# Five rooms instead of three for the first loads, and the low parts of x and of two weight groups summed by TensorE

## The chip, the cores and the metric

The kernel runs on one core of one Trainium2 chip. The metric is the device time of one execution in microseconds (us), the median of the timed runs. The profile is that of one execution, recorded by the hardware profiler.

## The reference

```python
def _attn_ref(q, k, v, alpha):                  # each (4, 8, 768, 48): batch, heads, time, head size
    state = np.zeros((B, H, D, D))
    for t in range(S):
        state = alpha[:, :, t, :, None] * state + np.einsum('bhd,bhe->bhde', k[:, :, t], v[:, :, t])
        y[:, :, t] = np.einsum('bhd,bhde->bhe', q[:, :, t], state)
...
def reference(...):
    x = np.ascontiguousarray(attn_out.transpose(0, 2, 1, 3)).reshape(B * S, H * D)   # (3072, 384)
    h = x @ w_in                                # w_in (384, 2048), float64
    g = np.maximum(0.01 * h, h)
    return (g @ w_out).astype(np.float32)       # w_out (2048, 384), float64
```

## The kernel before

**Two stages that overlap.** The attention is computed in 24 units: 4 batches by 6 time blocks of 128 tokens. The feed-forward part (FFN) has 16 weight groups `f` of 128 hidden columns and 8 token blocks `i` of three units each. `attention(0, AHEAD)` issues the first nine units (AHEAD = 9) ahead of the FFN; the other fifteen are spread between the FFN's matrix products later on. The rows below call the first nine units the head.

**A unit.** Its alpha, q, k and v (192 KB each) come by SP's DMA queue. TensorE transposes alpha, q and k (`transposed`, L280: four matmuls each, which write a PSUM bank of one of two kinds, `a` and `b`, in turn). VectorE (DVE) makes running products of alpha (L314, L320) and scales q (L339, `qs`) and k (L347, `ks`). TensorE makes the scores (`scores`, L356): for each of four head pairs one matmul on the rows 0 to 47 into one bank and one on the rows 64 to 111 into another, 16 records of a matmul in all, because a plain float32 matmul leaves two records. ScalarE (ACT) copies the two banks to `sm` (L366) and GpSimd (POOL) masks them (L367). `k_tokens` (L380) transposes `ks`. `outputs` adds old state times q (L395, from unit 4 on) and values times masked scores (L401) into a bank `y`, and makes the new key-value products (`kv`, L412). ACT rounds `y` to the high part of x (L418, `xh`, type float32r) and DVE subtracts it to give the low part (L419, `xl`).

**The weights.** `converting(f)` turns a group of float64 weights, read as pairs of 32-bit words, into a high part `hi` and a low part `lo` of float32r: two ACT operations (L245, L254) and six DVE operations, of which the last three form `val - hi` (L260), the remaining bits `rest` (L262) and `lo = rest + val` (L265). The first three groups are converted within the head, each behind the marks in the tables AFTER and BEGIN; the others run between the FFN's products.

**The FFN.** `ffn_in` (L493) is nine matmuls of 384 columns into a bank `ph` (hi by xh, hi by xl, lo by xh for three row blocks), then ACT and DVE work on the result; `ffn_out` (L520) is nine matmuls for each block and group.

**What sets the order.** A tile scheduler orders each engine's instructions; `behind(...)` and `put(...)` pin some to others. Each of alpha, q and k has two rooms in SBUF and a third in `spare` for the head's units, and the values have three rooms (NV). `load_next` issues the load of the unit that takes a room as soon as the room's user has been transposed; `load_values(u + NV)` stands at the end of `outputs(u)`. SP issues its transfers in order, and a transfer whose room is not free yet holds all those behind it. The table LOADS puts the weights of the first groups between them.

Of the kernel before, what the change touches and what calls it, by code (L numbers as in the profile page):

```python
# [9 lines left out]
F32 = mybir.dt.float32  # L10
F32R = mybir.dt.float32r
I32 = mybir.dt.int32
U32 = mybir.dt.uint32
I64 = mybir.dt.int64
AF = mybir.ActivationFunctionType
ALU = mybir.AluOpType
# [6 lines left out]
def gated_linear_attn_ffn(ctx, tc, q, k, v, alpha, w_in, w_out, out):  # L23
    nc = tc.nc
# [3 lines left out]
    P = 128  # L28
# [23 lines left out]
    NL = 2, 2, 2  # L52
    NV = 3
    NBITS, NPW, NRAW = 2, 1, 4
    T4 = 4
    RUN = T4 * D
    PITCH = RUN + GAP
    AHEAD = 3 * UPB
    LAG = 3
    SOON, EARLY = 2, 3  # L60
    LEAD = 8
# [29 lines left out]

    spare = pieces("spare", F32, *[(NP * PITCH,)] * 3)
    x_sb, = pieces("large", F32R, (3 * (NG + 1), 2, TB))
# [18 lines left out]
    def places(u, i):  # L112
        return loads_sb[i] + [spare[i]] if u < AHEAD else loads_sb[i]

# [3 lines left out]
    def load_next(u, i):  # L118

        for n in range(u + 1, u + 4):  # L120
            if n < NU and n - len(places(n, i)) == u:
                load(n, i)
# [4 lines left out]
    def load(u, i):  # L127
# [16 lines left out]
        for a in range(4):  # L144
# [4 lines left out]
            )  # L149

    def load_values(u):
        if u >= NU:
            return
        if u >= AHEAD and later is not None:
# [3 lines left out]
        made["v", u] = nc.sync.dma_start(  # L158
            vals_sb[u % NV].rearrange("t (h d) -> t h d", h=H),
            v[b, :, tb * C:(tb + 1) * C, :].rearrange("h t d -> t h d"),  # L160
# [4 lines left out]
    for i in (0, 1, 2):  # L165
        for t in places(0, i):
            nc.vector.memset(by_token(t)[:, :, D:], 1.0)
    for n in range(3):
        for i in range(3):
            load(n, i)  # L170
        if n < NV - 1:
            load_values(n)

# [7 lines left out]
    keep_warm(6)  # L181
    make_identity(nc, ident)
    nc.gpsimd.memset(mask, 1.0)
    nc.gpsimd.affine_select(
# [41 lines left out]
    def converting(f, ordered=False):  # L226
# [31 lines left out]
        put(ordered, "DVE", lambda: nc.vector.tensor_scalar(pw, bits, -0x800000, None, ALU.bitwise_and))  # L258
        yield
        put(ordered, "DVE", lambda: nc.vector.tensor_tensor(val, val, hi.bitcast(F32), ALU.subtract))  # L260
        yield
# [123 lines left out]
    def outputs(u):  # L385
        tb, b = units[u]
        i, j = divmod(u, UPB)
        pe, qs, ktok = live[u][:3]
        V, W = vals_sb[u % NV], state[b]
        at = i % 3 * (NG + 1)  # L390
# [16 lines left out]
        if tb < NC - 1:  # L407
            kv = bank()[:, 0:NP * D].rearrange("d (p e) -> d p e", p=NP)
            for p in range(NP):
                for s, lo, m in ((0, 0, HB), (1, HB, D)):  # L410
# [3 lines left out]
                    )  # L414
        load_values(u + NV)
        live[u] = pe, kv
        xh, xl = (x_sb[0:BR, at:at + NP, n, j * C:(j + 1) * C] for n in (0, 1))
        made["xh", u] = nc.scalar.copy(xh, y[0:BR])  # L418
        made["x", u] = nc.vector.tensor_tensor(xl, y[0:BR], xh.bitcast(F32), ALU.subtract)  # L419

# [133 lines left out]
    for n, _ in enumerate(st):  # L554
        if n == 2:
            load_values(NV - 1)
        while LOADS and LOADS[0][0] in made:
# [188 lines left out]
```

## Time and profile before

| what | value |
|---|---|
| timed runs | 530.58, 530.69, 531.53 us; median 530.69 us |
| span of the profiled execution | 530.9 us |
| TensorE (PE) busy | 518.5 us, 98% |
| VectorE (DVE) busy | 379.0 us, 71% |
| ScalarE (ACT) busy | 230.7 us, 43% |
| GpSimd (POOL) busy | 62.6 us, 12% |
| DMA | 46.64 MB in all, mean 88 GB/s |

The span runs from the first to the last instruction of the profiled execution; it lies 0.2 us above the median of the timed runs, so what is added to or taken from the span can be added to or taken from the time. The ends of matmuls are modelled, so busy time of TensorE overstates its work where matmuls overlap; the times at which they start are recorded. PEld is TensorE's loading of weights, which overlaps its matmuls.

### The profile page before, as it was taken

To read this page: it belongs to the slowest core of one execution; us is meant where nothing else is said; L and a number is where in the kernel's file an instruction comes from. 1 tells how busy PE (TensorE), PEld (TensorE's weight loads), DVE (VectorE), ACT (ScalarE), POOL (GpSimd) and SP (SyncE) were. 2 spreads that over 40 slices of the span, in tenths; PEclk is the share of its full clock that TensorE was granted. 3 is DMA by queue.
4 is the path that set the end of the run, shared out by engine and by line. 5 is a ranking of instruction groups with operands and counts; after the bars stand their busy time and mean duration, and the time that the engine had idled before them with its cause. 6 is when DMAs were issued, how large, how long until landed. Compare 5 with 4: busy or idle time off the path is not lost.

```text
span 530.9 us, 9962 instructions
## 1 busy us (share of the span) xinstructions
PE 518.5 (98%) x3778; PEld 500.0 (94%) x3778; DVE 379.0 (71%) x695; ACT 230.7 (43%) x489; POOL 62.6 (12%) x143
## 2 busy tenths in 40 slices
PE   8997999999999999999999999999999999999995
PEld 7886999999999999999999999999999999999995
DVE  6998899999999997777577586585786534333331
ACT  2764855555534444444334444345344444333331
POOL 4554500000000111100101101101010000000000
PEclk9998999999999999999999999999999999999998
DMA  9999975545726533552251431433201000101001
GB/s 144 168 175 170 229 172 133 131 122 141 170 45 184 127 84 81 102 134 49 60 111 30 112 83 44 92 74 86 54 15 25 31 16 1 23 1 44 1 0 51
DMA packets 92982, 46.64 MB, mean 88 GB/s; under 512 B 57856, under 2 KB 90112, under 8 KB 92928
## 3 DMA queue, kind: packets, MB, share of 16 engines
q1 hardware_dynamic: 92928, 45.93, 39.5%
q8 instruction: 32, 0.52, 0.4%
q14 instruction: 22, 0.18, 0.1%
HBM read 38.83 MB, written 4.72 MB: 82 GB/s over the span
## 4 chain that ended last, share of the span: by engine, by line
PE 87%; DVE 7%; DMA 4%; issue 1%; SPq 0%; DVEq 0%; ACT 0%
PE ph L493 35%; PE b L520 32%; PE a L356 4%; PE a L401 3%; PE a L520 3%; DMA small<-in_v_dram 3%; PE a L395 3%; PE a L412 2%; PE b L401 1%; PE a L380 1%; PE b L280 1%; DMA small<-in_alpha_dram 1%; DVE pw L262 1%; DVE gl L505 1%; DVE t L499 1%
## 5 line engine op out<-in xcount | busy, mean ns | idle before, releaser
L493 PE MATMUL ph<-large,w 128*128 128x384 f32 x1152 | 226.6, 338 | 0.5 <-DVE t L499 0.5
L493 PEld LDWEIGHTS ph<-large,w 128*128 128x128 f32 x1152 | 200.1, 188 | 2.8 <-DVE t L499 1.1
L520 PE MATMUL b<-w,gh 128*128 128x384 f32 x672 | 168.9, 340 | 0.0
L499 DVE TENSOR_TENSOR t<-ph,t 128x384 f32<-128x384 f32 x128 | 70.7, 553 | 79.1 <-ACT t L496 78.9
L520 PEld LDWEIGHTS b<-w,gh 128*128 128x128 f32 x672 | 119.4, 188 | 2.1 <-issue 0.4
L496 ACT ACTIVATE t<-ph 128x384 f32<-128x384 f32 x128 | 62.5, 489 | 128.2 <-PE ph L493 128.2
L501 ACT CAST gh<-t 128x384 fp32r<-128x384 f32 x128 | 65.7, 513 | 119.6 <-DVE t L499 119.6
L520 PE MATMUL b<-w,gl 128*128 128x384 f32 x336 | 107.4, 335 | 0.0
L505 DVE TENSOR_TENSOR gl<-t,gh 128x384 fp32r<-128x384 f32 x128 | 70.9, 554 | 34.3 <-ACT gh L501 34.2
L520 PEld LDWEIGHTS b<-w,gl 128*128 128x128 f32 x336 | 62.6, 188 | 0.0
L367 POOL TENSOR_SCALAR_AFFINE_SELECT sm<-sm 128x512 f32<-128x512 f32 x33 | 23.1, 712 | 207.8 <-ACT sm L366 207.8
L356 PEld LDWEIGHTS a<-qs,ks 48*128 48x128 f32 x312 | 24.1, 188 | 5.1 <-issue 4.2
L356 PE MATMUL a<-qs,ks 48*128 48x128 f32 x312 | 28.7, 285 | 0.0
L289 DVE STREAM_TRANSPOSE ks<-small 128x512 f32<-128x512 f32 x15 | 16.7, 1123 | 14.6 <-PE a L380 14.6
L324 POOL COPY pe<-pc 128x4 f32<-128x4 f32 x24 | 4.8, 202 | 163.7 <-DVE pc L314 163.7
L373 POOL TENSOR_TENSOR small<-us,pe 48x192 f32<-48x192 f32 x40 | 22.4, 560 | 1.5
L314 DVE TENSOR_TENSOR_SCAN pc<-e,small 128x128 f32<-128x128 f32 x60 | 20.4, 401 | 0.0
L366 ACT COPY sm<-a 128x512 f32<-128x512 f32 x24 | 14.0, 583 | 14.0 <-PE b L356 12.9
L520 PE MATMUL a<-w,gh 128*128 128x384 f32 x96 | 19.6, 337 | 0.0
L320 DVE TENSOR_TENSOR_SCAN rc<-e,small 128x511 f32<-128x511 f32 x15 | 19.1, 1276 | 0.2
L401 PE MATMUL a<-sm,small 128*48 128x128 f32 x256 | 17.7, 277 | 0.0
L254 ACT CAST w<-bits 128x768 fp32r<-128x768 f32 x16 | 13.4, 838 | 8.4 <-DVE bits L251 7.8
(92 smaller groups left out, 554.4 us busy)
## 6 DMA issues: line engine op xcount, KB each, us to landing
raw<-in_moe_w_out_dram SPq DMA_DIRECT2D x16, 384.0 KB, 3.8
small<-in_v_dram SPq DMA_DIRECT2D x24, 192.0 KB, 3.7
raw<-in_moe_w_in_dram SPq DMA_DIRECT2D x32, 144.0 KB, 4.0
out_dram<-o SPq DMA_DIRECT2D x24, 192.0 KB, 2.0
small<-in_alpha_dram SPq DMA_DIRECT2D x32, 96.0 KB, 2.3
small<-in_q_dram SPq DMA_DIRECT2D x30, 96.0 KB, 2.4
small<-in_k_dram SPq DMA_DIRECT2D x30, 96.0 KB, 2.2
small<-in_alpha_dram SPq DMA_DIRECT2D x30, 80.0 KB, 2.4
```

Of the source, the lines that this page charges most:

```text
L314: nc.vector.tensor_tensor_scan(pc[:, p, :], aT[:, p, :], ones.broadcast_to([P, C]), 1.0, ALU.mult, ALU.mult)
L320: nc.vector.tensor_tensor_scan(flat[2][:, NP * C - 2::-1], flat[0][:, NP * C - 1:0:-1], flat[1][:, NP * C - 2::-1], last, ALU.mult, ALU.add)
L356: nc.tensor.matmul(ss[s][:, p, :], ks[lo:lo + D, p, :], qs[lo:lo + D, p, :], start=True, stop=True)
L367: made["mask", u] = nc.gpsimd.affine_select(out=sm[s], in_=sm[s], compare_op=ALU.is_ge, fill=0.0, base=0, pattern=[[0, NP], [1, C]], chann ...
L373: nc.gpsimd.tensor_tensor(*scalings.pop(0))
L401: nc.tensor.matmul(y[lo:lo + m, p, :], V[:, c:c + m], masked[u][s][:, p, :], start=not tb and p == 0, stop=p == NP - 1, skip_group_check=True,
L493: nc.tensor.matmul(ph, w_in_of(f, wn, g), xt[:, g, :], start=n == 0, stop=n == 3 * NG - 1)
L496: put(ordered, "ACT", lambda: nc.scalar.mul(t, ph, 0.01))
L499: put(ordered, "DVE", lambda: nc.vector.tensor_tensor(t, ph, t, ALU.max))
L501: put(ordered, "ACT", lambda: nc.scalar.copy(gh, t))
L505: made["gl", i, f] = put(ordered, "DVE", lambda: nc.vector.tensor_tensor(gl, t, gh.bitcast(F32), ALU.subtract))
L520: product = nc.tensor.matmul(po[j], gt[:, js], w_out_of(f, wn), start=f == 0 and n == 0, stop=f == NF - 1 and n == 2)
```

## The change

The nine units' alpha, q and k get three spare rooms each (NS), so five rooms, and the values four more (NVS), so seven. At the start the loads of five units are issued in place of three; `values(u)` chooses a value room. `minus`, a negative identity of type float32r, is made on POOL. For the head's units the low part of x is no longer subtracted by DVE: TensorE adds `minus` times `xh` into the bank `y`, and ACT copies what is left. For the weight groups 0 and 1 (SUMS = 2) `lo` is summed by TensorE in two halves of 384 columns into a bank `ph`: identity times `val`, `minus` times `hi`, identity times `rest`, and ACT copies the sum. The two identity products are plain float32 matmuls, the product with `minus` is float32r. DVE sets the constant columns of six more rooms.

```diff
--- before.py
+++ after.py
@@ -51,12 +51,14 @@
 
     NL = 2, 2, 2
     NV = 3
+    NS, NVS = 3, 4
     NBITS, NPW, NRAW = 2, 1, 4
     T4 = 4
     RUN = T4 * D
     PITCH = RUN + GAP
     AHEAD = 3 * UPB
     LAG = 3
+    SUMS = 2
     SOON, EARLY = 2, 3
     LEAD = 8
     SL = 8 * UPB
@@ -89,7 +91,9 @@
     state, vals_sb, rest = rest[:B], rest[B:B + NV], rest[B + NV:]
     loads_sb = [[rest.pop(0) for _ in range(n)] for n in NL]
 
-    spare = pieces("spare", F32, *[(NP * PITCH,)] * 3)
+    spare = pieces("spare", F32, *[(H * HB,)] * (3 * NS), *[(DM,)] * NVS)
+    spare_sb = [[spare.pop(0) for _ in range(NS)] for _ in range(3)]
+    minus, = pieces("minus", F32R, (P,))
     x_sb, = pieces("large", F32R, (3 * (NG + 1), 2, TB))
 
     w_sb = {}
@@ -110,14 +114,14 @@
         return tc.issue_after(made[key].ins) if key in made else nullcontext()
 
     def places(u, i):
-        return loads_sb[i] + [spare[i]] if u < AHEAD else loads_sb[i]
+        return loads_sb[i] + spare_sb[i] if u < AHEAD else loads_sb[i]
 
     def loaded(u, i):
         return places(u, i)[u % len(places(u, i))]
 
     def load_next(u, i):
 
-        for n in range(u + 1, u + 4):
+        for n in range(u + 1, u + 3 + NS):
             if n < NU and n - len(places(n, i)) == u:
                 load(n, i)
 
@@ -148,6 +152,15 @@
                 src[b, a // 2::2, ts, :].rearrange("p (j t) d -> j p (t d)", t=T4)[:, :, off:],
             )
 
+    def values(u):
+        rooms = vals_sb + spare if u < AHEAD else vals_sb
+        return rooms[u % len(rooms)]
+
+    def load_more_values(u):
+        for n in (u + NV, u + NV + NVS):
+            if (n < AHEAD) == (n > u + NV):
+                load_values(n)
+
     def load_values(u):
         if u >= NU:
             return
@@ -156,7 +169,7 @@
             return
         tb, b = units[u]
         made["v", u] = nc.sync.dma_start(
-            vals_sb[u % NV].rearrange("t (h d) -> t h d", h=H),
+            values(u).rearrange("t (h d) -> t h d", h=H),
             v[b, :, tb * C:(tb + 1) * C, :].rearrange("h t d -> t h d"),
         )
 
@@ -165,11 +178,10 @@
     for i in (0, 1, 2):
         for t in places(0, i):
             nc.vector.memset(by_token(t)[:, :, D:], 1.0)
-    for n in range(3):
+    for n in range(2 + NS):
         for i in range(3):
             load(n, i)
-        if n < NV - 1:
-            load_values(n)
+        load_values(n)
 
     idle = ps_h.tile([P, 512], F32, name="ph")
 
@@ -180,6 +192,7 @@
 
     keep_warm(6)
     make_identity(nc, ident)
+    nc.gpsimd.tensor_scalar(minus, ident, -1.0, None, ALU.mult)
     nc.gpsimd.memset(mask, 1.0)
     nc.gpsimd.affine_select(
         out=mask, in_=mask, compare_op=ALU.is_ge, fill=0.0, base=0,
@@ -257,6 +270,15 @@
         rest = pw.bitcast(F32)
         put(ordered, "DVE", lambda: nc.vector.tensor_scalar(pw, bits, -0x800000, None, ALU.bitwise_and))
         yield
+        if f < SUMS:
+            nc.vector.scalar_tensor_tensor(rest, low.bitcast(U32), 2.0 ** -52, rest, ALU.mult, ALU.mult)
+            for cs in (slice(0, DM), slice(DM, 2 * DM)):
+                ps = ps_h.tile([P, 512], F32, name="ph")[:, 0:DM]
+                nc.tensor.matmul(ps, ident, val[:, cs], start=True, stop=False)
+                nc.tensor.matmul(ps, minus, hi[:, cs], start=False, stop=False)
+                nc.tensor.matmul(ps, ident, rest[:, cs], start=False, stop=True)
+                made["w", f] = nc.scalar.copy(lo[:, cs], ps)
+            return
         put(ordered, "DVE", lambda: nc.vector.tensor_tensor(val, val, hi.bitcast(F32), ALU.subtract))
         yield
         put(ordered, "DVE", lambda: nc.vector.scalar_tensor_tensor(
@@ -386,7 +408,7 @@
         tb, b = units[u]
         i, j = divmod(u, UPB)
         pe, qs, ktok = live[u][:3]
-        V, W = vals_sb[u % NV], state[b]
+        V, W = values(u), state[b]
         at = i % 3 * (NG + 1)
         y = banks4()
 
@@ -412,11 +434,15 @@
                     made["kv", u] = nc.tensor.matmul(
                         kv[lo:lo + m, p, :], ktok[:, p, lo:lo + m], V[:, h * D:(h + 1) * D], start=True, stop=True
                     )
-        load_values(u + NV)
+        load_more_values(u)
         live[u] = pe, kv
         xh, xl = (x_sb[0:BR, at:at + NP, n, j * C:(j + 1) * C] for n in (0, 1))
         made["xh", u] = nc.scalar.copy(xh, y[0:BR])
-        made["x", u] = nc.vector.tensor_tensor(xl, y[0:BR], xh.bitcast(F32), ALU.subtract)
+        if u < AHEAD:
+            nc.tensor.matmul(y[0:BR], minus[0:BR, 0:BR], xh, start=False, stop=True, skip_group_check=True)
+            made["x", u] = nc.scalar.copy(xl, y[0:BR])
+        else:
+            made["x", u] = nc.vector.tensor_tensor(xl, y[0:BR], xh.bitcast(F32), ALU.subtract)
 
     def next_state(u):
         tb, b = units[u]
@@ -553,7 +579,8 @@
     loaded_f = converted = 0
     for n, _ in enumerate(st):
         if n == 2:
-            load_values(NV - 1)
+            for u in range(2 + NS, NV + NVS):
+                load_values(u)
         while LOADS and LOADS[0][0] in made:
             key, f, part = LOADS.pop(0)
             with behind(*key):
```

The scheduler moves other instructions with it. The names in the rows are those of the tiles that an instruction writes and reads.

TensorE at the scores of unit 2 before the change (L356 scores, L380 transposes of `ks`, L280 transposes of the next unit's q and k):

```order
L356 MATMUL a<-qs,ks 128x128
L356 MATMUL b<-qs,ks 128x128
L356 MATMUL a<-qs,ks 128x128
L356 MATMUL b<-qs,ks 128x128
L356 MATMUL a<-qs,ks 128x128
L356 MATMUL b<-qs,ks 128x128
L356 MATMUL a<-qs,ks 128x128
L356 MATMUL b<-qs,ks 128x128
L380 MATMUL a<-small,ks 128x112 x4
L280 MATMUL a<-small 128x128 x4
L280 MATMUL b<-small 128x128 x4
```

The same place after it (L378 scores, L402 transposes of `ks`, L302 transposes of loads, L442 the new product with `minus`):

```order
L302 MATMUL b<-small,spare 128x128 x4
L378 MATMUL a<-qs,ks 128x128 x4
L402 MATMUL a<-small,ks 128x112 x4
L378 MATMUL b<-qs,ks 128x128 x4
L302 MATMUL a<-small,spare 128x128 x2
L442 MATMUL b<-large,minus 112x512
L302 MATMUL a<-small,spare 128x128 x2
```

The scores of this unit no longer alternate between the banks `a` and `b`: four go to `a`, then the transposes of `ks`, then four to `b`. The units 2, 4 and 6 stand like this in the changed kernel; in the one before, all nine alternate. The product with `minus` stands between transposes of the next unit.

TensorE in unit 6 after the change, where the sums of weight group 0 stand (L277 identity times `val`, L278 `minus` times `hi`, L279 identity times `rest`, L434 key-value products):

```order
L378 MATMUL a<-qs,ks 128x128 x4
L402 MATMUL a<-small,ks 128x112 x4
L302 MATMUL a<-small,spare 128x128 x2
L378 MATMUL b<-qs,ks 128x128 x4
L442 MATMUL b<-large,minus 112x512
L302 MATMUL a<-small,spare 128x128 x2
L277 MATMUL ph<-bits,small 128x384 x2
L278 MATMUL ph<-w_681,minus 128x384 x2
```

The rows L277 to L279 are new; L279 of this group follows the key-value products. Those of group 1 stand in unit 7 (L277) and between the scores of unit 8 (L278, L279). The nine matmuls `ffn_in(0, 0)`, which ran between the scores of units 7 and 8, now follow those of unit 8. From there on TensorE's order is the same as before, and the program has 21 TensorE instructions more.

SP's queue before the change, from the alpha of unit 8 to the values of units 7 and 8 (L139 loads, L158 values, L209 and L213 weights, L449 the gather of x):

```order
L139 DMA spare<-in_alpha_dram 128x8x48
L449 DMA large<-large 16x3x768
L158 DMA small<-in_v_dram 128x8x48
L213 DMA raw<-in_moe_w_out_dram 128x384
L209 DMA raw<-in_moe_w_in_dram 48x3x128 x2
L209 DMA raw<-in_moe_w_in_dram 16x3x128
L139 DMA spare<-in_k_dram 128x8x48
L209 DMA raw<-in_moe_w_in_dram 16x3x128
L139 DMA spare<-in_q_dram 128x8x48
L158 DMA small<-in_v_dram 128x8x48 x2
```

The corresponding stretch after it, from the weights of group 0 to the values of units 7 and 8 (L143 loads, L171 values, L222 and L226 weights):

```order
L226 DMA raw<-in_moe_w_out_dram 128x384
L143 DMA spare<-in_alpha_dram 128x8x48
L222 DMA raw<-in_moe_w_in_dram 48x3x128 x2
L222 DMA raw<-in_moe_w_in_dram 16x3x128 x2
L171 DMA spare<-in_v_dram 128x8x48
L226 DMA raw<-in_moe_w_out_dram 128x384
L222 DMA raw<-in_moe_w_in_dram 48x3x128
L143 DMA spare<-in_k_dram 128x8x48
L143 DMA spare<-in_q_dram 128x8x48
L222 DMA raw<-in_moe_w_in_dram 48x3x128
L222 DMA raw<-in_moe_w_in_dram 16x3x128 x2
L143 DMA spare<-in_alpha_dram 128x8x48
L171 DMA small<-in_v_dram 128x8x48 x2
```

The first row with values (L158, L171) in each piece is that of unit 6. Before, it stands behind the alpha of unit 8 and two gathers of x, and waits for the room of unit 3. Now it stands ahead of the k and q of unit 7, of the alpha of unit 8 and of all gathers, and its room is one that no earlier unit uses. The values of units 7 and 8 stay the last loads but the k and q of unit 8.

## Rows read from the trace of the kernel before

**Rows 1.** The page, part 1: busy us, share of the span, instructions.

```profile
PE 518.5 (98%) x3778; PEld 500.0 (94%) x3778; DVE 379.0 (71%) x695; ACT 230.7 (43%) x489; POOL 62.6 (12%) x143
```

**Rows 2.** Windows in the head: busy us (instructions), granted clock, DMA share, GB/s.

```profile
core 0: us, PE busy (x) PEld busy (x) DVE busy (x) ACT busy (x) POOL busy (x), PEclk, DMA share, GB/s
13.00:26.00 13.00, 12.87 (x177) 10.44 (x176) 12.49 (x29) 9.71 (x25) 7.07 (x17) 1.00 1.11 169
39.00:52.00 13.00, 9.55 (x112) 8.25 (x112) 11.73 (x24) 6.31 (x15) 7.26 (x11) 0.91 1.18 175
10.70:59.40 48.70, 44.73 (x552) 38.34 (x551) 44.89 (x92) 30.82 (x73) 25.21 (x50) 0.96 1.08 175
```

**Rows 3.** Chain of waits in the head: start us, us, what held the end.

```profile
3.04 5.20 DMA small<-in_alpha_dram
...
15.58 0.30 PE a L356
...
20.51 0.30 PE a L356
20.82 0.10 PE a L356
...
30.56 0.30 PE a L356
...
31.65 0.53 PE a L380 x4
...
59.46 0.30 PE b L356
```

**Rows 4.** Waits, 10.7 to 59 us: us in total, times, longest.

```profile
PE b L401 <- DMA small<-in_v_dram: 3.1, 2, 2.8
...
PEld b L401 <- POOL sm L367: 1.2, 4, 0.5
...
PEld b L280 <- DVE rc L320: 1.1, 2, 0.8
...
PEld a L356 <- DVE w L265: 0.4, 1, 0.4
...
PEld a L280 <- DVE us L432: 0.3, 1, 0.3
PEld b L395 <- DVE large L419: 0.3, 2, 0.2
```

**Rows 5.** Timeline, SP and PE: start us, us, [idle before, releaser].

```profile
41.45 0.54 SPq L158 DMA_DIRECT2D small<-in_v_dram  x1
...
49.92 2.79 SPq L158 DMA_DIRECT2D small<-in_v_dram  x2
...
49.98 0.42 PE L401 MATMUL b<-sm,small 128*48 128x128 f32 x1 [2.79 <-DMA small<-in_v_dram]
```

**Rows 6.** Windows of 2 us behind the longest wait, columns as in rows 2.

```profile
50.00:52.00 2.00, 2.00 (x27) 2.00 (x29) 1.26 (x5) 0.00 (x0) 0.19 (x1) 0.50 0.97 129
52.00:54.00 2.00, 2.00 (x25) 1.59 (x21) 1.21 (x2) 1.04 (x2) 0.00 (x0) 0.71 0.64 125
```

**Rows 7.** Chain of waits, pieces that give prices on TensorE.

```profile
57.14 0.87 PE b L395 x8
...
112.78 1.56 PE ph L493 x9
...
183.72 1.81 PE a L356 x16
```

**Rows 8.** Groups by form, 0 to 66 us: busy us, mean ns, idle before.

```profile
L419 DVE TENSOR_TENSOR large<-b,large 112x512 fp32r<-112x512 f32 x8 | 5.4, 673 | 0.8 <-ACT large L418 0.8
L418 ACT CAST large<-b 112x512 fp32r<-112x512 f32 x8 | 4.7, 585 | 11.3 <-PE b L401 11.3
L260 DVE TENSOR_TENSOR bits<-bits,w 128x768 f32<-128x768 f32 x2 | 2.3, 1157 | 0.0
L265 DVE TENSOR_TENSOR w<-pw,bits 128x768 fp32r<-128x768 f32 x2 | 1.9, 949 | 0.0
L254 ACT CAST w<-bits 128x768 fp32r<-128x768 f32 x2 | 1.7, 840 | 0.9 <-DVE bits L251 0.9
L167 DVE MEMSET spare<- 128x128 f32 x3 | 0.5, 165 | 0.0
```

**Rows 9.** Windows behind the head, columns as in rows 2.

```profile
78.00:91.00 13.00, 13.00 (x76) 12.81 (x75) 13.00 (x21) 7.25 (x13) 0.00 (x0) 1.00 0.51 125
156.00:169.00 13.00, 12.53 (x72) 12.21 (x71) 13.00 (x25) 4.60 (x11) 0.74 (x3) 1.00 0.59 156
```

## The prediction

> **What bounds the kernel now.** The page's first part comes first: TensorE is busy for 518.5 of 530.9 us, VectorE for 379.0 [rows 1]. So TensorE bounds the kernel as a whole, and the question is how much room its 12.4 us of idle time leave, and where. A share of the whole span says little about the head, which is all that the change touches, so the windows of the head come next. From 13 to 26 us TensorE is busy for 12.87 of 13 us, but VectorE for 12.49 too; from 39 to 52 us TensorE falls to 9.55 and VectorE stays at 11.73 [rows 2]. Two engines share the lead, then, and busy TensorE is a modelled figure. To decide between them I read the chain of waits. Apart from loads, it runs through TensorE: the scores of two neighbouring units start at 15.58 and 20.51 us, a cadence of 4.93 us, and the pieces between them are matmuls end to end [rows 3]. In the list of waits TensorE waits for VectorE only in small pieces: 1.1 us for the scan L320, 0.4 for L265, 0.3 for L432, 0.3 for L419 [rows 4]. The longest wait is one for a transfer: 2.79 us in unit 6, for its values, which SP issued at 41.45 us and TensorE could use at 49.98 [rows 5]. Behind it, after those idle 2.79 us, the granted clock reads 0.50, the lower of its two levels (1.2 GHz), for 2 us and 0.71, part lower and part upper level (2.4 GHz), for the next 2, while TensorE is busy throughout [rows 6]. From the L395 at 57.14 us [rows 7] the chain is TensorE's own products until the end of the stages read below.
>
> **What the change takes from TensorE's path.** (1) The wait for the values of unit 6, 2.8 us [rows 5]. They now have a room of their own and stand ahead of the second group's weights in SP's queue. The queue moves no faster: DMA carried 175 GB/s in this stretch and its share is 1.08 [rows 2], so what is moved ahead makes something else later, here the second group's weights and the gathers. Next late would be the values of units 7 and 8, issued last in both kernels (49.92 to 52.7 us [rows 5]); unit 7's outputs begin with the L395 at 57.14 us [rows 7], so I count no new wait. (2) The clock after that wait: at 0.50 and 0.71, 2 us of work count for 1.00 and 1.42, so 1.00 + 0.58 = 1.6 us [rows 6]. (3) The small waits for VectorE, 1.1 + 0.4 + 0.3 + 0.3 = 2.1 us, and what is left of the values' total, 3.1 - 2.8 = 0.3 [rows 4]: 2.4 us if all go. The 1.2 us for POOL's mask [rows 4] stay, since the mask is untouched. Together 6.8 us.
>
> **What it takes from VectorE.** Nine subtractions L419 of 0.673 us make 6.1, two L260 of 1.157 and two L265 of 0.949 make 4.2; six more memsets of 0.165 add 1.0 [rows 8]. That is 9.3 us less. The memsets run while the first alpha is on its way (5.20 us of transfer [rows 3]) and cost nothing; without that cover they would cost their 1.0. The relief itself counts only where TensorE waits for VectorE, which is term 3 and one later stage: from 78 to 91 us both engines are busy for all 13 us, and from 156 to 169 TensorE misses 0.47 while VectorE is full [rows 9]. A VectorE that enters this stage earlier gives back about that: 0.4 us.
>
> **What it adds to TensorE.** (4) Nine products with `minus`, 512 columns of float32r. Nine L493 of 384 columns, the same type, take 1.56 us, 0.1735 each [rows 7], hence 0.231 for 512 and 2.1 us in all. (5) Four halves of weight sums. The float32 products here are 384 columns wide, which no row shows. Four L395 of 128 float32 columns (eight records) take 0.87 us [rows 7], so 0.218 for 128 columns and 0.65 for 384; that is the upper bound. The lower is two records at the float32r price, 0.35. I take 0.65, since it comes from the same type. A half is 0.65 + 0.17 + 0.65 = 1.47, four are 5.9 us (lower bound 3.5). They can't hide: where they stand TensorE is already the chain. (6) The scores that no longer alternate. Alternating, unit 4's take from 30.56 to 31.65 us, 1.09 us, for 16 records [rows 3], since a matmul on rows 0 to 47 and one on rows 64 to 111 run side by side. A later unit's 16 that stand mostly in one bank at a time take 1.81 [rows 7]. The difference is 0.72; for a clean split of four and four I take 0.8, and three such units make 2.4 us. Bounds: 0 if transposes on other rows fill the gap, 1.09 a unit if nothing overlaps. (7) Changes of shape. The first score behind another shape takes 0.30 in place of 0.10 [rows 3], 0.2 each. Three split units have one change more each, 0.6; for `minus` among transposes of nearly its height I add 0.5 over nine. Bounds 0 and 1.5. Together 2.1 + 5.9 + 2.4 + 1.1 = 11.5 us.
>
> The Trainium skill, FP8 and Floating Point Precision, section TensorE Precision Notes, says that true FP32 takes four passes through the array. By that rule a float32 product of 384 columns would be four times a float32r one, an estimate of 0.69 us in place of 0.65, and the four halves 0.3 us dearer in all; the trace agrees, with 0.218 us for 128 columns against 4 x 0.058 from L493. The Trainium skill, TensorEngine Tiling (Array Packing), section Key Properties, says that changing the tiling mode drains TensorE and that different tiles can work in parallel. It speaks against term 6 as the rows do: the trace shows 1.09 against 1.81 us for the same scores.
>
> **What goes to ScalarE.** Nine copies of 512 columns at about 0.585 [rows 8] and four of 384 at most as long: 7.6 us more on 30.82 of 48.70 busy [rows 2]. It stays below the span of the head, so nothing is counted, but it works in order (a rival, below).
>
> **The sum.** 11.5 - 6.8 - 0.4 = +4.3 us. The profiled span of 530.9 becomes 535.2; it lies 0.2 above the median of the runs, so the time becomes **535.0**.
>
> **Rivals.** *Slower (535.0), TensorE bounds the head:* chance 0.64. With the float32 products at their lower bound (-2.4) it is 532.6, with full loss of overlap and dear changes (+0.9 +0.4) it is 536.3, and with the small waits kept (+2.4) 537.4: its own range is 532.4 to 537.5.
>
> *Faster: VectorE bounds the head.* For it: 12.49 of 13 us busy, and 44.89 against TensorE's 44.73 over the whole head [rows 2], while TensorE's figure is modelled. Then each of six units before the wait is shorter by 0.67 us, 4.0 in all, the new products hide in TensorE's true idle time, and the wait (2.8), the clock (1.6) and the later stage (0.4) come on top: 8.8. The sums, behind 50 us, still cost 3.5 at least. So -5.3, **525.4**. Against it: the chain names TensorE, and so little waiting for VectorE is on record [rows 4]. It decides once the units' cadence falls below 4.7 us. Chance 0.14.
>
> *No change:* the sums at 3.5 (-2.4) and the split scores overlapped by transposes (-2.4): 4.3 - 4.8 = -0.5, **530.2 to 531.5**. For it: no row shows either form. Against: L395 is the same type. Chance 0.11.
>
> *Slower still: ScalarE's order.* The group's `hi` (0.840 [rows 8]) and a copy of `xl` now stand ahead of the score copies of units 6 to 8. Each delays score copy, mask and outputs by up to 0.84 + 0.585 = 1.4 us; three times that is 4.2 more than the first case: **539.2**. It decides once TensorE's wait for the mask L367, 1.2 us now [rows 4], passes 3. Against: ScalarE has some 18 us of idle in the head. Chance 0.11.
>
> **Chances.** A measurement of this kernel can tell about 0.2%, 1.1 us, from no change. Faster by more (below 529.6): the second case, 0.14. Within: the third, 0.11, and a sliver of the first, 0.01. Slower (above 531.8): 0.63 + 0.11 = 0.74. The range must leave out no more than 2 in 10: it takes the first and the third case and the lower part of the last, 530.0 to 538.5, and leaves out the faster case and the upper half of the last.
>
> **What would show each step right or wrong.** In the changed kernel's profile: no wait of unit 6 for its values and a granted clock of 1.00 from 48 to 54 us (terms 1, 2); L442 starts followed 0.23 us later by the next matmul (4); about 1.5 us for the three products of each half (5); the scores of units 2, 4 and 6 spread over about 1.9 us of TensorE's own (6); the scores of unit 8 starting later than 59.46 us [rows 3] by 0 to 2 us, and `ffn_in(0, 0)`, which had its place before them, behind; VectorE clearly below 12 of 13 us from 13 to 26. The prediction is wrong if the units' cadence falls by more than 0.3 us with TensorE still full, for then VectorE was the bound, or if a new wait for a load appears early, since five units' loads now compete for the same 175 GB/s [rows 2].

## The result and the profile after

The changed kernel takes 538.83 us (median of 4 runs, 538.02 to 538.98) against 531.11 us before (530.58 to 532.03): a ratio of 1.0142, 95% interval 1.0127 to 1.0157. It is slower, as forecast, but by 7.7 us between the medians where 4.3 were forecast, and just outside the range (538.5).

The page of the changed kernel, part 1, to be read beside [rows 1]:

```profile
PE 528.6 (98%) x3807; PEld 507.3 (94%) x3807; DVE 370.8 (69%) x688; ACT 238.1 (44%) x502; POOL 59.4 (11%) x144
```

TensorE is busy for 10.1 us more, VectorE for 8.2 less. The windows of the head (columns as in [rows 2]) show TensorE ahead of VectorE by 2 to 5 us in each, where the two shared the lead before:

```profile
13.00:26.00 13.00, 12.99 (x153) 10.45 (x152) 10.15 (x21) 9.77 (x26) 6.10 (x15) 1.00 1.23 169
26.00:39.00 13.00, 13.00 (x150) 10.87 (x150) 9.22 (x20) 7.76 (x19) 6.81 (x16) 1.00 1.05 192
39.00:52.00 13.00, 13.00 (x133) 10.55 (x128) 11.12 (x23) 9.12 (x20) 5.93 (x12) 1.00 1.05 188
52.00:65.00 13.00, 12.58 (x117) 9.33 (x115) 7.55 (x15) 7.36 (x15) 3.62 (x6) 1.00 0.98 208
...
156.00:169.00 13.00, 13.00 (x76) 13.00 (x76) 13.00 (x23) 4.28 (x9) 0.55 (x2) 1.00 0.24 58
```

TensorE is full from 13 to 52 us at the upper level of its clock (granted 1.00), where from 39 to 52 us it had 9.55 of 13 us at 0.91 before [rows 2]. The hole of unit 6 and the slow clock behind it [rows 5, 6] are gone. What the matmuls still wait for from 10 to 72 us is short, and no load is in the list (us in total, times, longest):

```profile
PE ph L277 <- DVE bits L264: 0.4, 1, 0.4
PE a L378 <- DVE ks L369: 0.3, 1, 0.3
```

The last of the FFN's L519 stands at 524.5 us; its counterpart before stood at 518.8. First the row of L493 before, then that of L519 after (min/median/max of one in ns, first and last start in us):

```profile
L493 PE MATMUL ph<-large,w x1152: 333/336/445, 54.4 to 518.8; 128*128 128x384 f32 x192
```

```profile
L519 PE MATMUL ph<-large,w x1152: 333/336/446, 66.7 to 524.5; 128*128 128x384 f32 x192
```

The chain of waits of the changed kernel (start us, us, what), at the split scores of unit 4 and at the sums of group 0, to be read beside [rows 3, 7]:

```profile
32.04 1.08 PE a L378 x8
33.12 0.53 PE a L402 x4
33.65 1.08 PE b L378 x8
...
35.11 0.23 PE b L442
...
48.90 1.29 PE ph L277 x4
50.19 0.34 PE ph L278 x2
50.53 0.59 PE a L434 x14
51.13 1.49 PE ph L279 x4
```

Two float32 products of 384 columns take 1.29 us, 0.65 each, the value taken from L395. A split unit's scores take 2.16 us of TensorE in place of 1.09: the upper bound.

**What the times stand on.** In every run the time lies some 1.7 us above the span. In the 89 runs of the kernel before that were timed beside the experiments, the median span is 529.5 us, and only 3 reach 530.9, the span of the profile that the prediction was worked on. That profile was of one of the longest executions; its distance of 0.2 us to the median, which the text ahead of the prediction and the prediction state, set the span of one execution against the times of others. Below, each experiment is set against the median of the kernel before on the same chip.

### The profile page after: what moved, and what is told of

Its sections match the earlier page's. It is cut to its first block, busy times and chain, and to the rows that moved or that the text cites. A ratio compares the mean times of both kernels' runs of the same rounds, so it can differ in the third digit from the quotient of the medians.

```text
span 537.2 us, 10028 instructions
## 1 busy us (share of the span) xinstructions
PE 528.6 (98%) x3807; PEld 507.3 (94%) x3807; DVE 370.8 (69%) x688; ACT 238.1 (44%) x502; POOL 59.4 (11%) x144
## 4 chain that ended last, share of the span: by engine, by line
PE 97%; DVE 1%; issue 0%; ACT 0%; DVEq 0%
PE ph L519 38%; PE b L546 33%; PE a L546 5%; PE a L378 5%; PE a L423 3%; PE a L417 3%; PE b L423 2%; PE a L434 2%; PE a L402 2%; PE b L302 1%; PE b L378 1%; PE a L302 1%; PE ph L191 1%; PE b L417 1%; PE ph L277 1%; PE ph L279 1%
## 5 line engine op out<-in xcount | busy, mean ns | idle before, releaser
L519 PE MATMUL ph<-large,w 128*128 128x384 f32 x1152 | 225.3, 337 | 0.0
L519 PEld LDWEIGHTS ph<-large,w 128*128 128x128 f32 x1152 | 200.8, 188 | 1.1 <-PE a L423 0.2
L389 POOL TENSOR_SCALAR_AFFINE_SELECT sm<-sm 128x512 f32<-128x512 f32 x33 | 20.6, 634 | 204.0 <-ACT sm L388 204.0
L378 PEld LDWEIGHTS a<-qs,ks 48*128 48x128 f32 x312 | 23.9, 187 | 5.5 <-issue 4.5
L378 PE MATMUL a<-qs,ks 48*128 48x128 f32 x312 | 28.6, 285 | 0.3 <-DVE ks L369 0.3
L395 POOL TENSOR_TENSOR small<-us,pe 48x192 f32<-48x192 f32 x40 | 20.5, 512 | 1.5
```

Of the source, the lines that this page charges most:

```text
L378: nc.tensor.matmul(ss[s][:, p, :], ks[lo:lo + D, p, :], qs[lo:lo + D, p, :], start=True, stop=True)
L389: made["mask", u] = nc.gpsimd.affine_select(out=sm[s], in_=sm[s], compare_op=ALU.is_ge, fill=0.0, base=0, pattern=[[0, NP], [1, C]], chann ...
L395: nc.gpsimd.tensor_tensor(*scalings.pop(0))
L519: nc.tensor.matmul(ph, w_in_of(f, wn, g), xt[:, g, :], start=n == 0, stop=n == 3 * NG - 1)
```

## The experiments

| what runs | us | before, same chip | ratio, 95% interval |
|---|---|---|---|
| e1 rooms alone | 534.59 | 531.43 | 1.0057, 1.0041 to 1.0074 |
| e2 rooms and sums | 535.27 | 531.43 | 1.0068, 1.0053 to 1.0084 |
| e3 rooms and minus | 534.13 | 531.43 | 1.0050, 1.0034 to 1.0066 |
| e4 changed, scores alternate | 539.57 | 531.43 | 1.0157, 1.0140 to 1.0173 |
| e5 rooms, first FFN products late | 532.03 | 531.46 | 1.0018, 1.0008 to 1.0028 |
| e6 rooms, gathers on ScalarE's queue | 563.03 | 531.46 | 1.0594, 1.0570 to 1.0618 |
| e7 sums alone | 535.38 | 531.46 | 1.0083, 1.0062 to 1.0105 |
| e8 minus alone | 533.86 | 531.46 | 1.0053, 1.0035 to 1.0071 |
| e9 before once more | 531.44 | 530.86 | 1.0009, 0.9994 to 1.0024 |
| e10 as e5, no low x | 533.41 | 530.86 | 1.0044, 1.0027 to 1.0062 |
| e11 as e5, weights' low parts on POOL | 532.21 | 530.86 | 1.0024, 1.0008 to 1.0039 |
| e12 before, weights' low parts on POOL | 532.60 | 530.86 | 1.0031, 1.0020 to 1.0042 |
| e13 changed, sums cut | 533.99 | 530.93 | 1.0062, 1.0045 to 1.0080 |
| e14 changed, minus cut | 534.00 | 530.93 | 1.0057, 1.0037 to 1.0077 |
| e15 before, weight group 1 late | 535.21 | 530.93 | 1.0081, 1.0061 to 1.0102 |
| e16 changed, weight group 1 late | 538.83 | 530.93 | 1.0145, 1.0124 to 1.0167 |
| e17 changed, both cut | 531.42 | 531.22 | 1.0009, 0.9996 to 1.0021 |
| e18 before, first FFN products late | 531.49 | 531.22 | 1.0009, 0.9996 to 1.0022 |

**The parts, e1 to e3.** Each is the changed kernel with parts undone:

```diff
-    SUMS = 2
+    SUMS = 0                # e1, e3
...
-        if u < AHEAD:       # the low part of x on TensorE
+        if u < 0:           # e1, e2
```

> The changed kernel with the rooms alone: five for alpha, q, k, seven for v; the low parts of x and of all weights are subtracted by VectorE as before. Theory (TensorE bounds the head, its new products are the loss): the wait for the values of unit 6, the slow clock behind it and little else go, -4 to -5.5 us, so 525 to 527 us. Rival (five units' loads crowd the same DMA, or the next load is late at once): 530 us or more, with a new wait for a load in the first units.

> Rooms, and the sums of weight groups 0 and 1 on TensorE; the low parts of x stay with VectorE. Theory: the rooms' time plus four halves of about 1.5 us, so e1 + 6 us, 531 to 533. Rival (VectorE's relief of 4.2 us counts, or the products fit into idle time): e1 + 0 to 2 us.

> Rooms, and the nine products with minus on TensorE; the weight sums stay with VectorE. The scores of units 2, 4 and 6 stand split in this one too. Theory: the rooms' time plus 9 x 0.24 for the products, 3 x 1.07 for the split scores and about 1 for changes of shape, so e1 + 6 us. Rival (the split costs nothing, or VectorE's relief of 6.1 us pays for it): e1 + 0 to 2 us.

The rooms alone were to be 4 to 5.5 us faster; they are 3.2 us slower. The theory that only TensorE's products were the loss fell with that. The waits of e1 (us in total, times, longest) name a new one, and its timeline of SP's queue the place:

```profile
PE ph L519 <- DMA large<-large: 3.3, 1, 3.3
```

```profile
49.04 2.66 SPq L475 DMA_DIRECT2D large<-large  x4
```

The gathers of x stand behind all the head's loads now, and the first nine FFN matmuls, which in e1 kept their place ahead of unit 8's scores, wait for them. e2 and e3 lie 0.7 us above and 0.5 us below e1, not 6 above; the intervals overlap, so neither can be told from it. In e2 the FFN products stand behind unit 8's scores, so that the gathers' wait is covered; in e3 they stand ahead of them, and it is partly paid (1.4 us in its list of waits).

**The split scores, e4.** The order within a unit's scores is pinned:

```diff
+        prev = None
...
-                nc.tensor.matmul(ss[s][:, p, :], ks[lo:lo + D, p, :], qs[lo:lo + D, p, :], start=True, stop=True)
+                with tc.issue_after(prev.ins) if prev is not None else nullcontext():
+                    prev = nc.tensor.matmul(ss[s][:, p, :], ks[lo:lo + D, p, :], qs[lo:lo + D, p, :], start=True, stop=True)
```

> The changed kernel with the scores of each unit held in their written order, so that all nine head units alternate between the banks a and b. Theory (scores that alternate run in pairs): 3 x 1.07 = 3.2 us less than the changed kernel, 535.0 to 536. Rival (the split only filled the time in which the second bank was still held by the low part of x): no gain, 538 to 539, with waits of the scores on a ScalarE copy.

539.57, 8.1 us over the kernel before, where the changed kernel lies 7.7 over it: no gain. The split is not wholly undone: in units 2, 4 and 6 the transposes of `ks` (L404 there) still stand behind the first of the eight matmuls, so that a unit gains 0.6 us and not 1.07. Up to unit 5 there was a gain. In the two chains of waits (that of e4 first, then that of the changed kernel) unit 5's scores start 1.3 us earlier:

```profile
38.30 0.30 PE a L380
```

```profile
39.56 0.30 PE a L378
```

It is lost again behind unit 6, where TensorE waits 1.4 us for VectorE's scan:

```profile
PE b L302 <- DVE rc L342: 1.4, 1, 1.4
```

So the split has its price in its own unit, and taking that much of it away did not move the end. Why the order around units 6 to 8 takes it back was not separated further.

**The place of the FFN and of the gathers, e5, e6 and e18.** e5 is e1, and e18 is the kernel before, with both first FFN calls issued behind `k_tokens(8)`; e6 is e1 with the first three gathers issued by ScalarE:

```diff
-        if n in STARTS:                                     # e5, e18
+        for _ in STARTS if n == 69 else ():
             i, f = items[len(gs)][:2]
-            with behind(*STARTS[n]):
+            with behind("kt", 8):
...
-            made["g", i] = nc.sync.dma_start(               # e6
+            made["g", i] = (nc.scalar if i < 3 else nc.sync).dma_start(
```

> The rooms alone, with the first nine FFN matmuls behind the scores of unit 8 as in the changed kernel; all else as in e1. Theory (in e1 TensorE waited at these nine, because the gathers of x stand behind all the head's loads in SP's queue): that wait of some 3.5 us goes, the rooms show their gain: 528 to 530 us, 4 to 6 less than e1. Rival (the unit's VectorE chain bounds it there anyway): 533 to 535 us, as e1.

> The rooms alone, with the gathers of the first three token blocks issued on ScalarE's queue, so that no load stands ahead of them; the first nine FFN matmuls stand where they stood before. The scores of unit 4 are split in this one. Theory (the gathers' place in SP's queue is what made the rooms slower): the wait at the first FFN matmuls goes, 529 to 531 us. Rival (crowding of the DMA itself): 533 to 535 us, the gather lands late from the other queue too.

> The kernel before, with its first nine FFN matmuls behind the scores of unit 8, as they stand in the changed kernel. Theory (they filled time in which TensorE had nothing else): 531 to 532.5, no gain. Rival (they hold the scores of unit 8 up, and VectorE behind them): 528.5 to 530.

e5 takes 2.6 us off e1: the gathers' wait was most of what the rooms lost. But it is still not faster than before (0.6 us slower, 1.0018), nor than e18 (0.3 us slower, 1.0009), which has the same place for the FFN and three rooms. The rooms gain nothing even where the gathers are covered. e18 shows something else besides: in its profile, of 528.8 us, TensorE waits only 0.3 us for values, with three rooms too, where the profile of before had 3.1 [rows 4]. e6 says nothing on its question: ScalarE stood still at the first gather (start us, us, [idle before, releaser]) until a load of k landed, and the masks and TensorE with it:

```profile
52.93 0.58 ACT L388 COPY sm<-a 128x512 f32<-128x512 f32 x1 [26.82 <-DMA spare<-in_k_dram]
```

**Each product by itself, e7 and e8.** The kernel before with one of the two edits, and the `minus` that it needs:

```diff
+    minus, = pieces("minus", F32R, (P,))
...
+        if f < 2:           # e7: the lines of the change behind "if f < SUMS"
...
+        if u < AHEAD:       # e8: the lines of the change that make xl
```

> The kernel before, with the sums of weight groups 0 and 1 on TensorE alone: three rooms, low part of x on VectorE. Theory (TensorE's new products count, less what VectorE's relief gives back): 531.4 + 1 to 2.5 = 532.4 to 534 us. Rival (all 6.2 us of new products count): 537 to 538 us.

> The kernel before, with the nine products with minus alone (the scores of units 2, 4 and 6 are split in it). Theory (9 x 0.24 of products, 1.6 for each of the three units whose second bank of scores waits): 531.4 + 2 + 4 = 537 us, less what the late values of unit 6 would have cost anyway (up to 4), so 533.5 to 537. Rival (hidden in the wait for the loads): 530.5 to 532.

3.9 us for products that take 6.2 us of TensorE, and 2.4 us for nine products of 0.23 and three splits of 1.07, 5.3 together. Part of each seems to lie in time in which TensorE would otherwise wait. e2 and e3, which have the rooms as well, lie 3.8 and 2.7 us over the kernel before: hardly more, or less, than the 3.2 that the rooms alone lose there. All of it together costs 7.7, more than 3.9 + 2.4 = 6.3. That the second part finds less waiting time left would explain this; no run shows it by itself.

**Is the profile of before typical, e9.** The kernel before, unchanged:

> The kernel before once more, for a second profile. Theory (the profile that the prediction was built on is of an execution at the upper end of the runs, with a longer wait and a slower clock than most): a span of 529 to 530 us, clock 0.997 to 0.999, unit 6's wait for its values under 2.2 us. Rival (the profile is typical): span 530.9, clock 0.994, wait 2.8 us.

Its profiled execution was a long one again: 531.4 us, with 1.5 us of waiting for the values and 1.5 for alpha:

```profile
PE b L280 <- DMA spare<-in_alpha_dram: 1.5, 1, 1.5
PE b L401 <- DMA small<-in_v_dram: 1.5, 1, 1.5
```

So the wait is not that of one load. Which load is late, and by how much, changes between executions of one program; the spans of the 89 runs reach from 527.7 to 531.5 us. e9 does not decide its question: its span and clock (531.4 us, 0.994) are the rival's, its wait for the values is the theory's. What tells that the profile of before was a long execution is the 89 spans.

**Is VectorE the bound with the rooms, e10 to e12.** In the chain of e5 VectorE's work stood nearly end to end from 41 to 56 us. Some of its longer pieces (start us, us, what):

```profile
42.42 0.90 DVE bits L264
...
43.57 1.19 DVE rc L342
...
45.26 0.55 DVE pw L271
...
46.33 1.38 DVE bits L282
47.70 1.18 DVE pw L284
```

That made VectorE the suspect. e10 takes the nine subtractions out of e5; e11 and e12 give four operations of the weights to POOL:

```diff
+    nc.gpsimd.memset(x_sb.bitcast(F32)[:, :, 1, :], 0.0)    # e10
-        else:
+        elif u >= AHEAD:
             made["x", u] = nc.vector.tensor_tensor(xl, y[0:BR], xh.bitcast(F32), ALU.subtract)
...
+        low_on = nc.gpsimd if f < 2 else nc.vector          # e11, e12
+        put(ordered, "DVE", lambda: low_on.tensor_tensor(val, val, hi.bitcast(F32), ALU.subtract))
...
+        made["w", f] = put(ordered, "DVE", lambda: low_on.tensor_tensor(lo, rest, val, ALU.add))
```

> The rooms with the FFN's first matmuls late (as e5), and the head's low parts of x left out (set to zero once, so nine VectorE operations of 0.67 us fall away and TensorE does nothing in their place; the output lacks these parts). Theory (with the rooms VectorE bounds units 5 to 8): four units are shorter by 0.67 each, 2.7 us less than e5, 529 to 529.7. Rival (TensorE or the loads bound them): 531.5 to 532.3, as e5.

> As e5, with the two operations that subtract and add the low parts of weight groups 0 and 1 on POOL in place of VectorE (four operations, 4.2 us of VectorE). Theory (VectorE bounds units 6 and 7): up to 4 us less than e5, 528 to 530. Rival (POOL's masks queue behind the slower operations, and TensorE waits for them): 532 us or more.

> The kernel before with the same four operations on POOL, without the rooms. Theory (there the values of unit 6 arrive late, so VectorE's relief has nothing to shorten until they are there): within 1 us of before, 530.5 to 531.5. Rival (VectorE bounds units 6 and 7 here too): 528 to 530.

None is faster, and e12, at 1.7 us over the kernel before, is slower than both of its forecasts; why was not separated. e10 does not decide its question, because of two side effects of its own. POOL spends 3.94 us at the start on setting the low parts to zero, and the identity that TensorE needs comes after it, so that the first scores start at 12.03 us where they start at 10.32 in e5. And SP issues the q of unit 7 at 42.66 us, behind all of weight group 1, where e5 issues it at 39.06. From the scores of unit 0 to those of unit 6 e10 is 1.0 us faster than e5 (30.51 against 31.49 us); then TensorE waits for that q:

```profile
PE b L303 <- DMA spare<-in_q_dram: 4.3, 1, 4.3
```

In e11 it waits 1.9 us for loads of q and 1.1 us for loads of k. The chain of e5 may have been right for its one execution, but where VectorE has less to do, TensorE is found waiting for loads instead.

**TensorE or the loads, e13 to e17.** e13, e14 and e17 cut products from the changed kernel; e15 and e16 move the loads of weight group 1 behind the attention's, in the kernel before and in the changed one:

```diff
-                nc.tensor.matmul(ps, ident, val[:, cs], start=True, stop=False)          # e13, e17
-                nc.tensor.matmul(ps, minus, hi[:, cs], start=False, stop=False)
-                nc.tensor.matmul(ps, ident, rest[:, cs], start=False, stop=True)
+                nc.tensor.matmul(ps, minus, hi[:, cs], start=True, stop=True)
...
-            nc.tensor.matmul(y[0:BR], minus[0:BR, 0:BR], xh, start=False, stop=True, skip_group_check=True)   # e14, e17
...
-    LOADS = [(("v", 4), 0, 0), (("v", 5), 0, 1), (("v", 6), 1, None), (("g", 1), 2, None), (("v", 8), 3, None)]
+    LOADS = [(("v", 4), 0, 0), (("v", 5), 0, 1), (("v", 8), 1, None), (("v", 8), 2, None), (("v", 8), 3, None)]   # e15, e16
```

> The changed kernel without the eight float32 products of the weight sums (only minus times hi and the copies stay, so the low parts of groups 0 and 1 are wrong in it). Theory (TensorE is full through the whole head): the eight products' 8 x 0.65 = 5.2 us come back, 538.8 - 5.2 = 533.6. Rival (the loads set the end of the head): 1 to 2 us come back, 537 to 538, and TensorE waits for a load in units 6 to 8.

> The changed kernel without the nine products with minus (ScalarE copies y itself as low part, which is wrong in it). The scores alternate in all units of this one. Theory (TensorE is full): 9 x 0.24 and 3 x 1.07 come back, 538.8 - 5.4 = 533.4. Rival (loads, or ScalarE's copies): 536 to 538.

> The kernel before with the loads of weight group 1 (0.8 MB) behind all the attention's loads of the first nine units; nothing else changed. Theory (the rate of the loads sets when units 6 to 8 can run): the values of unit 8 come some 4 us earlier, TensorE's wait in units 6 to 8 shrinks; group 1 is converted later, which its first use has slack for: 528 to 530. Rival (VectorE or TensorE bounds those units, or the late group 1 is waited for): 531 or more.

> The changed kernel with the loads of weight group 1 behind the attention's. Theory (TensorE, not the loads, bounds the changed kernel): no gain, 538 to 540. Rival (loads bound it too): 534 to 537.

> The changed kernel without the eight float32 products of the sums and without the nine products with minus (both low parts are wrong in it): the rooms and VectorE's relief remain. Theory (two bounds: the products fill TensorE, and behind them the rate of the loads holds units 7 and 8): not the sum of both cuts, 529, but 531 to 532.5, with a wait of 2 to 5 us for a load of unit 7 or 8. Rival (TensorE alone): 529 us.

e13 and e14 lie 3.1 us over the kernel before, the changed kernel 7.7: each cut alone gives 4.7 us back, of the 5.2 and 5.4 that the products and the splits take. So in the changed kernel TensorE is the bound, if by little: e4 took 1.3 us of its work away up to unit 5, and a wait for VectorE took them back. e16 agrees: loads in another order change nothing there. Both cuts together do not give 9.3 us but 7.5, down to the time of the kernel before. The list of waits of e17 and its chain have the reason:

```profile
PE b L300 <- DMA spare<-in_q_dram: 2.9, 1, 2.9
```

```profile
39.51 6.13 DMA spare<-in_q_dram
```

This is the q of unit 7. It lands at 45.65 us, where TensorE had been idle since 42.92. In the kernel before SP issued it at 38.49 us and it landed 4.7 us later, at 43.2. In the new order the values of unit 6 (192 KB) and the first 528 KB of weight group 1 stand ahead of it, which stood behind it before, and it comes 2.5 us later. The values of unit 6 come 8.8 us earlier, at 41.0 us in place of 49.8. The new wait brings its own slow clock (windows of e17, columns as in [rows 2]):

```profile
46.00:48.00 2.00, 2.00 (x16) 2.00 (x15) 1.43 (x3) 1.31 (x4) 1.62 (x3) 0.79 0.86 178
48.00:50.00 2.00, 2.00 (x12) 1.67 (x12) 0.20 (x1) 0.00 (x0) 0.00 (x0) 0.50 1.23 194
50.00:52.00 2.00, 2.00 (x37) 1.95 (x36) 1.82 (x7) 0.41 (x1) 0.38 (x2) 0.86 1.30 177
```

At 0.79, 0.50 and 0.86, 6 us of work count for 4.3, so 1.7 us are lost behind 2.9 of waiting: 4.6 together, as much as the 2.8 + 1.6 = 4.4 that were to be gained.

The rate of the loads in the first 50 us hardly depends on the rooms; the windows from 4 to 50 us of the kernel before, of the changed one and of e17, in this order:

```profile
4.00:50.00 46.00, 41.13 (x485) 34.90 (x484) 41.71 (x87) 25.48 (x61) 23.58 (x49) 1.00 1.15 175
```

```profile
4.00:50.00 46.00, 45.53 (x478) 38.31 (x476) 35.78 (x76) 27.91 (x67) 20.88 (x48) 1.00 1.17 180
```

```profile
4.00:50.00 46.00, 42.53 (x489) 36.85 (x488) 37.25 (x79) 29.34 (x69) 23.11 (x50) 0.97 1.16 181
```

Nine units of 768 KB and two weight groups of 768 KB (8 bytes for each of 2 x 128 x 384 weights) are 8.65 MB; at 0.18 MB a us that is 48 us, an estimate, whatever the number of rooms. More rooms change which load comes late, and hardly how much has come by a given time. The last values of the head are issued by SP at 49.92 us before [rows 5]; in the changed kernel SP issues them at 43.81, but the k and q of unit 8 behind them:

```profile
43.81 1.73 SPq L171 DMA_DIRECT2D small<-in_v_dram  x2
45.64 2.06 SPq L143 DMA_DIRECT2D spare<-in_k_dram  x1
47.80 0.80 SPq L143 DMA_DIRECT2D spare<-in_q_dram  x1
```

No run has the rooms without the products and with the q of unit 7 ahead of weight group 1, so it is not shown whether another order of the same loads would have brought a gain.

e15 was to gain by taking 0.8 MB out of the way and lost 4.3 us: the first operation of group 1's conversion then waits for its load on ScalarE, ahead of a unit's score copies, and TensorE for those. So this test of the loads was spoilt by a wait that it made itself:

```profile
PE b L395 <- ACT sm L366: 3.3, 1, 3.3
```

No version beat the kernel before; e17 and e18, the nearest, can't be told from it.

## Why the prediction was right in its direction and too low

**The step that failed** is "so I count no new wait", on which the 2.8 and 1.6 us of terms 1 and 2 rest. The prediction had the row for it, 175 GB/s at a DMA share of 1.08 [rows 2], and said itself that what is moved ahead makes something else later. It then named the second group's weights, the gathers and the values of units 7 and 8, and not the k and q of unit 7, which the new order also puts back. e17 shows what stands in its place. It keeps the rooms and all of VectorE's relief, and of the products only the four of `minus` and `hi` (0.17 us each). It is 0.2 us slower than the kernel before (interval of the ratio 0.9996 to 1.0021) where 6.8 us, and 0.4 more later, were counted as gain. The wait for the values of unit 6 is gone in it; the wait for the q of unit 7 and the slow clock behind that take 4.6 us. e10 and e14 wait for the same q (4.3 and 1.8 us), e1 for a gather (3.3 us).

**Term 3** was too large as well. Its 2.1 us of waits for VectorE are rows of PEld, the loading of weights, which overlaps the matmuls. The matmuls themselves waited for VectorE for 0.5 us in the same stretch of the kernel before:

```profile
PE b L280 <- DVE rc L320: 0.5, 1, 0.5
```

**The reference was a long execution.** 2.8 us of wait and 1.6 us of slow clock belong to a profile of 530.9 us of span, which 86 of 89 runs stayed below. So up to 1.4 us of what was to be gained (530.9 - 529.5) may not be there in the median execution; of one of median span there is no trace. "0.2 above the median" took time and span for the same measure; in the runs they are 1.7 us apart. In the profiles alone the change is 537.2 - 530.9 = 6.3 us, and some 7.5 between the median spans.

**The products, terms 4 to 7, 11.5 us.** Their sizes were about right. Most float32 products of 384 columns took 0.65 us, the value taken (term 5); the estimate from the Trainium skill's FP8 and Floating Point Precision, section TensorE Precision Notes, was 0.69. `minus` took 0.23 to 0.24 in all but two places (term 4). The split cost 1.07 a unit, where 0.8 was taken (term 6). The changes of shape (term 7) were not measured by themselves. What failed is "they can't hide": the products cost 7.7 us over the kernel before in the changed kernel against 0.2 in e17, so 7.5, and the other 4 us replace waiting and slow clock such as e17 has. Two errors in the same place cancelled in part, a gain that isn't there and a cover that is: 7.2 us of gain that isn't there and 0.2 of loss, less 4 us of cost too many, make the 3.4 us by which 4.3 fell short of 7.7. The direction came out for the reason that was given, the new products on a full TensorE; that the number came as near as it did is partly luck.

**The rivals.** The one on VectorE fell. It let each of six units be shorter by 0.67 us, 4.0 together. e17 has all of VectorE's relief and nearly none of the products, and from the scores of unit 0 to those of unit 6 it takes 30.69 us where the kernel before took 31.22. The one on no change fell too: the sums cost their upper price, and transposes did not fill the split scores. The one on ScalarE gave nearly the measured number (539.2) by luck, with the wrong mechanism: it needed TensorE's wait for the mask to pass 3 us, and the changed kernel has less of it than before:

```profile
PEld b L423 <- POOL sm L389: 0.7, 4, 0.2
```

**The signs named beforehand.** No wait for unit 6's values and a granted clock of 1.00: seen. The next matmul 0.23 us behind the start of L442: not seen as worded, it starts 0.31 to 0.33 us behind it in eight of nine places, though the chain gives L442 its 0.23. 1.5 us for three products: seen, 1.29 + 0.34 + 1.49 = 3.1 us for the two halves of group 0. The scores of a split unit over 1.9 us: 2.16. Scores of unit 8 0 to 2 us later than 59.46: they start at 62.87, 3.4 later. VectorE clearly below 12 of 13 us: seen. A shorter cadence with TensorE full: not seen, 4.92 us between the scores of units 1 and 2 where it was 4.93. An early new wait for a load: none in the changed kernel. The later recovery was larger than 0.4: of the 1152 matmuls of the FFN's first product the 101st starts 7.0 us later than before and those from the 401st on 5.7 us later, so 1.3 us come back. e13, e14 and e17 show 1.3 to 1.5 us there too, e1 and e5, which do not have the relief, none.

## What to carry to other kernels

Before a wait for a transfer is counted as won, go through every load that the new order puts back, add up the bytes that now stand ahead of it, divide by the rate of that stretch, and compare with the time at which it is wanted. If the queue already moves at its rate, more rooms only move the wait to another tile. Where three limits lie within a few us of each other (here TensorE, VectorE and the loads), relief of one can be worth next to nothing and load on another less than its length, so cut each part out by itself and all of them together. Compare spans with spans, and look at how the spans of many executions scatter before a profile's waits are put into a sum.

## What the runs showed that was not expected

With a gather as ScalarE's own DMA issue (e6), ScalarE stood still for 26.8 us, and the releaser named is a k load of SP's queue, which the gather does not read. What ties the two together was not found. And the place of a wait for loads differs between executions of the same program (values of unit 6 for 2.8 us in one, values 1.5 and alpha 1.5 in another), while the rate of the transfers from 4 to 50 us, 175 to 181 GB/s, was nearly the same in the kernels in which it was read.
